# A new plan of instruction order for a linear-attention and feed-forward kernel on one Trainium2 core

## The chip, the cores and the metric

The kernel runs on one core of one Trainium2 chip. The metric is the device time of one execution in microseconds (us). Most executions of one kernel agree within a few tenths of a per cent, but chips differ by about one per cent: in the four sets of rounds used here, on three chips or more, the kernel before took 191.03, 193.21, 192.01 and 192.41 us. Kernels are compared by a ratio: the mean time of one kernel's fast runs over the mean time of the other kernel's fast runs of the same rounds on the same chip. It is not quite the ratio of the medians that are quoted. A run more than 1.5% above the fastest of its kernel counts as slow and stays out of the ratio. Each ratio has a 95% interval. All "spans" are those of one profiled execution.

## The reference, cut to what matters

```python
# r, k, v: (4 batches, 8 heads, 768 steps, 48), float32; w, u: (8, 48)
for t in range(S):
    cur = u * k_t (outer) v_t
    y[t] = r_t @ (state + cur)
    state = w * state + k_t (outer) v_t
x = y as (3072 tokens, 384)
h = x @ w_in                  # (384, 2048)
out = relu(h) ** 2 @ w_out    # (2048, 384)
```

The kernel cuts time into chunks of 128 steps: 6 chunks by 4 batches make 24 **units**, chunk by chunk. Per unit it scales r and k by powers of the decay, transposes both, forms masked scores (eight matrix products), y (scores times v plus r times the old state), and the new state. Two units make a **pair** for the feed-forward part: 8 groups of six w_in products and twice 8 groups of two w_out products for each of 12 pairs.

## The kernel before

The kernel lists every operation with its engine, an assumed cost and a key. A function plays the list through in an imaginary clock and so fixes the order in which each engine's queue receives its instructions. "S" is the sync queue, which issues loads, DMA transposes and stores; "D" is the DMA engines; "T", "V", "A", "P" are TensorE, VectorE (DVE), ScalarE (ACT) and GpSimd (POOL). The clock in this plan is only the kernel's own idea of time; the chip runs by semaphores.

```python
        cost = o.eng[e]                      # in schedule(): one shared port of V and P
        if e == "V" and o.port and last["P"] is not None and last["P"].end > s and last["P"].port:
            cost += 0.4
...
    NLOAD, NPADS = 8, 4                      # 8 buffers each for k, r and v tiles
    NT = 10                                  # from unit 10 on, transposes go by DMA
    NDVE = 6                                 # from unit 6 on, the products are GpSimd's alone
...
        full = [(loads[-4], 0.0)] if len(loads) >= 4 else []
        behind = [(loads[-1].go, 0.0)] if loads else []
        q[nm + "_go"] = op(f"ld_{nm}{n}", {"S": 0.45}, PACE * (n - AHEAD), full + behind + [gate], f, takes=[q["_" + nm]], lat=0.8)
        q[nm] = op(f"{nm}{n}", {"D": 0.88}, PACE * (n - AHEAD), [q[nm + "_go"]], lambda e: None, lat=0.75)
...
    w_ops = []                               # four units, then w_in and w_out by turns, then the rest
    for i in range(len(PIECES) - 1):
        for which in ("in", "out"):
            w_ops.append(weights(i, which, w_ops[-3] if len(w_ops) >= 3 else units[2]["vt"]))
...
            q["go_t"] = op(                  # DMA transpose of the scaled r and k of a unit
                f"go_t{n}", {"S": 0.5}, K + 1, [q["rw"]],
                lambda e, T=T: nc.sync.dma_start_transpose(...), takes=[X["rkT"]], uses=[X["krp"]], lat=0.8)
...
                q["smo"] = op(f"smo{n}", both(0.96, 0.48), K + 5, [q["sma"]],      # decay of the state: 128 x 384
                              tt(lambda sm=sm: SM(sm), lambda sm=sm: SM(sm), lambda: wc, ALU.mult), uses=[sm], port=True)
...
                o_go = op(f"go_x{q['n']}", {"S": 0.5}, PACE * q["n"] + 4.4, [q["yb"]],   # DMA transpose of y into xt
                          lambda e, XT=XT, i=i, q=q: nc.sync.dma_start_transpose(...), ...)
            o_m = op(f"m1.{j}.{f}", {"T": 0.655}, key, o_xt + [o_win[f]], m1, ...)       # a w_in group
                prev[i] = op(f"m2.{j}.{i}.{f}", {"T": 0.325}, key + LAG + 0.2 * i, ...)  # a w_out group
            o_st = op(f"st{q['n']}", {"S": 0.5}, KM + PACE * (L + i) - 30, [o_o], ...)   # store, sync queue only
```

## Time and profile before

| | before |
|---|---|
| time, median (lowest to highest) | 191.03 us (190.22 to 191.9) |
| span of the profiled execution | 188.4 us |
| first w_in product | 19.46 us |
| last w_in group starts | 181.74 us |
| TensorE's work, by the spacing of starts | 147.3 us, of it 143.8 after the first w_in product |
| TensorE without work after the first w_in product | 21.3 us |

A product is charged its own spacing in a dense row (0.109 us for one of w_in, 0.163 for one of w_out), and what is left between two starts is a hole. Half-speed clock counts as hole too. Two lines of the view of the waits (engine, line, tile, the releaser; then us in total, times, longest):

```profile
POOL krp L290 <- DMA kt<-in_k_dram: 8.9, 1, 8.9
PE bank L559 <- DMA xt<-yb: 3.5, 1, 3.5
```

The first is GpSimd standing still for unit 4's k, loaded behind all weights. The second is TensorE standing still at 94 us for the transposed y tile of unit 11.

### The profile page before, as it was taken

The numbers are of one execution on the slowest core, as the hardware profiler recorded it, in microseconds if no ns is written. First come the engines' busy times: TensorE is split into PE (matmuls) and PEld (weight loads), VectorE is DVE, ScalarE is ACT, GpSimd is POOL, SyncE is SP. The second block draws the span as 40 slices with busy tenths as digits, with TensorE's granted clock in tenths as the row PEclk, the third lists the DMA queues.
The fourth block names the chain that finished last, engine by engine and source line by source line (L and its number), as shares of the span: only waits on it lengthen the run. The fifth ranks groups of instructions, "written<-read, shape, count | busy, mean of one in ns | idle before, by whom it ended". The sixth has DMA issues, their size and how long they took to land.

```text
span 188.4 us, 4319 instructions
## 1 busy us (share of the span) xinstructions
PE 170.1 (90%) x1643; PEld 121.9 (65%) x1643; DVE 135.0 (72%) x229; ACT 110.2 (58%) x197; POOL 128.2 (68%) x144
## 2 busy tenths in 40 slices
PE   6997778869979999799839999999999999999992
PEld 2753555657767867577526767777777777777760
DVE  6579985569877777778605879788687776874741
ACT  4565654459787597567603645677565564464641
POOL 2588751089999989989908799999999993000000
PEclk9999999999999999999966999999999999999999
DMA  5999999999899999998894898406433424030202
GB/s 111 214 219 132 125 184 161 196 179 245 174 232 230 201 218 207 206 216 173 208 191 94 210 175 199 123 0 153 88 80 121 94 64 122 0 108 23 83 3 85
DMA packets 103256, 27.56 MB, mean 146 GB/s; under 512 B 96065, under 2 KB 103234, under 8 KB 103234
## 3 DMA queue, kind: packets, MB, share of 16 engines
q1 hardware_dynamic: 99088, 24.13, 58.4%
q0 software_dynamic: 4128, 3.15, 12.2%
q8 instruction: 13, 0.21, 0.5%
q14 instruction: 9, 0.07, 0.1%
q10 hardware_dynamic: 18, 0.00, 0.0%
HBM read 20.65 MB, written 4.72 MB: 135 GB/s over the span
## 4 chain that ended last, share of the span: by engine, by line
PE 54%; DMA 20%; POOL 13%; SPq 5%; issue 3%; DVE 2%; ACT 1%; POOLq 0%
PE bank L588 24%; PE bank L559 22%; DMA w_out_sb<-in_moe_w_out_dram 6%; POOL krp L290 5%; SPq L356 4%; DMA kt<-in_k_dram 4%; DMA w_in_sb<-in_moe_w_in_dram 3%; PE bank L483 3%; POOL rk L290 2%; POOL rku L290 2%; DMA vt<-in_v_dram 2%; DMA rt<-in_r_dram 2%; POOL dv L290 2%; DMA rkT<-krp 2%; PE bank L507 2%
## 5 line engine op out<-in xcount | busy, mean ns | idle before, releaser
L559 PE MATMUL bank<-xt,w_in_sb 128*128 128x256 bf16 x576 | 79.1, 276 | 6.7 <-DMA xt<-yb 3.5
L588 PE MATMUL bank<-w_out_sb,g 128*128 128x384 bf16 x384 | 81.2, 329 | 0.1
L579 ACT ACTIVATE g<-gr 128x512 bf16<-128x512 f32 x92 | 57.9, 630 | 36.9 <-DVE gr L571 36.1
L571 DVE TENSOR_SCALAR gr<-bank 128x512 f32<-128x512 f32 x73 | 50.4, 691 | 32.1 <-PE bank L559 27.3
L559 PEld LDWEIGHTS <-w_in_sb 128*128 128x128 bf16 x576 | 55.3, 99 | 21.8 <-DMA xt<-yb 3.9
L588 PEld LDWEIGHTS <-g 128*128 128x128 bf16 x384 | 34.4, 98 | 15.4 <-ACT g L579 0.6
L491 DVE TENSOR_TENSOR AT<-bank,smask 128x512 bf16<-128x512 f32 x48 | 30.8, 682 | 2.4 <-PE bank L483 1.9
L290 POOL TENSOR_TENSOR rk<-rt,kt 128x384 f32<-128x384 f32 x24 | 24.7, 1027 | 4.2 <-DMA rt<-in_r_dram 4.2
L290 POOL TENSOR_TENSOR krp<-kt,wk 128x384 bf16<-128x384 f32 x19 | 19.0, 1002 | 8.9 <-DMA kt<-in_k_dram 8.9
L290 POOL TENSOR_TENSOR krp<-rt,wr 128x384 bf16<-128x384 f32 x22 | 22.6, 1026 | 1.0 <-DVE krp L290 1.0
L295 ACT CAST vb<-vt 128x384 bf16<-128x384 f32 x24 | 12.3, 511 | 16.4 <-PE bank L507 9.6
L290 POOL TENSOR_TENSOR rku<-rk,ub 128x384 f32<-128x384 f32 x21 | 21.2, 1011 | 0.2
L290 POOL TENSOR_TENSOR dv<-vb,du 128x384 f32<-128x384 bf16 x20 | 17.0, 848 | 4.1 <-DVE du L422 4.1
L573 ACT ACTIVATE gr<-bank 128x512 f32<-128x512 f32 x23 | 13.7, 595 | 6.0 <-PE bank L559 5.5
L515 DVE TENSOR_TENSOR yb<-bank,dv 128x384 bf16<-128x384 f32 x24 | 13.3, 553 | 5.0 <-PE bank L507 4.1
L290 POOL TENSOR_TENSOR sm<-sm,wc 128x384 f32<-128x384 f32 x15 | 15.0, 999 | 1.7 <-DVE sm L290 1.6
L422 DVE TENSOR_REDUCE du<-rku 128x8 f32<-128x384 f32 x24 | 13.0, 543 | 0.5 <-POOL rku L290 0.4
L483 PE MATMUL bank<-rkT 48*128 48x128 bf16 x192 | 10.0, 222 | 2.6 <-DMA rkT<-krp 1.4
L507 PE MATMUL bank<-vb,AT 128*128 128x48 bf16 x192 | 11.5, 186 | 0.4 <-DVE AT L491 0.4
L507 PEld LDWEIGHTS <-AT 128*128 128x128 bf16 x192 | 10.0, 98 | 2.2 <-issue 1.1
L483 PEld LDWEIGHTS <-rkT 48*128 48x128 bf16 x192 | 5.7, 95 | 8.6 <-issue 4.1
L295 ACT CAST sb<-sm 128x384 bf16<-128x384 f32 x20 | 10.1, 505 | 1.7 <-DVE sm L290 1.5
(54 smaller groups left out, 137.8 us busy)
## 6 DMA issues: line engine op xcount, KB each, us to landing
kt<-in_k_dram SPq DMA_DIRECT2D x24, 192.0 KB, 3.7
rt<-in_r_dram SPq DMA_DIRECT2D x24, 192.0 KB, 3.6
vt<-in_v_dram SPq DMA_DIRECT2D x24, 192.0 KB, 3.7
out_dram<-osb SPq DMA_DIRECT2D x24, 192.0 KB, 2.4
w_in_sb<-in_moe_w_in_dram POOLq DMA_DIRECT2D x3, 384.0 KB, 6.6
w_out_sb<-in_moe_w_out_dram POOLq DMA_DIRECT2D x3, 384.0 KB, 7.0
w_in_sb<-in_moe_w_in_dram POOLq DMA_DIRECT2D x2, 192.0 KB, 4.6
w_out_sb<-in_moe_w_out_dram POOLq DMA_DIRECT2D x2, 192.0 KB, 4.3
```

The source lines that it names most:

```text
L290: return lambda e: NOW[e].tensor_tensor(dst(), a(), b_(), f)
L295: nc.scalar.copy(dst(), src())
L422: lambda e, T=T: nc.vector.tensor_reduce(T("du"), T("rku"), axis=mybir.AxisListType.X, op=ALU.add),
L483: nc.tensor.matmul(out=psv(at[i], NP, C)[:, p, :], lhsT=T("rkT")[rows, 1, p, :], rhs=T("rkT")[rows, 0, p, :], start=True, stop=True,)
L491: lambda e, T=T, i=i, x=x: nc.vector.tensor_tensor(T("AT")[:, i], psv(x, NP, C), smask[:, None, :].to_broadcast([128, NP, C]), ALU.mult),
L507: nc.tensor.matmul(out=t[:, p, i, :], lhsT=T("AT")[:, i, p, :], rhs=T("vb")[:, 2 * p + i, :], start=st is None, stop=True, skip_group_chec ...
L515: lambda e, T=T, y_p=y_p: nc.vector.tensor_tensor(T("yb"), psv(y_p, HD), T("dv").rearrange("t h d -> t (h d)"), ALU.add),
L559: nc.tensor.matmul(out=psv(h, 2, L * C)[:, z], lhsT=w_in_sb[:, kk, (2 * f + z) * 128 : (2 * f + z + 1) * 128], rhs=XT()[:, kk].rearrange(" ...
L571: nc.vector.tensor_scalar(dst, src, 0.0, None, ALU.max)
L573: nc.scalar.activation(dst, src, AF.Relu)
L579: nc.scalar.activation(dst, src, AF.Square)
L588: nc.tensor.matmul(out=psv(o_p, dm), lhsT=G()[:, 2 * f + z, i, :], rhs=w_out_sb[:, 2 * f + z, :], start=(f == 0 and z == 0), stop=(f == NH ...
```

## The change

The intent is to give each queue an order that the chip can follow without holes. The plan gets a model of DMA in phases (issue, transfer, completion), true queue costs, stalls for instruction fetches and an exclusive port for DVE and GpSimd; the order is then tuned by a table of 189 entries that override key, engine or earliest place of single operations. Beside that the kernel itself changes: w_in comes in one stretch and w_out in another, loads are paced by the scores of three units earlier, stores may go by ACT's queue, the state is stored densely, early decay tables lie in PSUM, and the u product uses full height. Smaller parts: DMA transposes begin with unit 8 instead of 10, the first two w_in groups of the first two pairs are split by unit, and TensorE starts with more products of zeros (48 instead of 19).

```diff
-def schedule(ops, depth, limits, free, away, warm_until):
+def schedule(ops, depth, limits, free, away, stalls, warm_until=0.0, cold=0.0):
...
+                if e == "V" and o.port:
+                    for a, b in heldP[-6:]:
+                        if s < b and s + cost > a:
+                            s = b                       # wait instead of paying for overlap
...
+        if o.dma is not None:
+            pre, xf, post = o.dma
+            x0 = max(s + pre, free["D"])
+            x1 = x0 + xf + sum(d for at, d in stalls if x0 <= at < x0 + xf)
...
-    NT = 10
-    NDVE = 6
+    NT = 8
+    NDVE, RUN = 24, 3
+    NUDGE = {
+        "vt0": (0.0, None, 5.57), "rt4": (0.0, None, 26.62), "vt8": (0.0, None, 51.18), ...   # (key, engine, earliest)
+        "m1.11.6": (0.0, None, 170.12), "m1.11.7": (0.0, None, 173.84),
+    }
+    FEED = (("units", 0, 4), ("in", 0, 5), ("units", 4, 6), ("out", 0, 5), ("units", 6, NU))
...
-        q[nm + "_go"] = op(f"ld_{nm}{n}", {"S": 0.45}, ...)
+        q[nm] = op(f"{nm}{n}", {"S": 0.58}, PACE * (n - AHEAD), deps, f, takes=[q["_" + nm]], lat=0.05, dma=(1.75, 0.92, 0.7))
...
-                f"go_t{n}", {"S": 0.5}, K + 1, [q["rw"]],
+                f"rkT{n}", {"S": 1.24}, K + 1, [q["rw"]],
...
-                q["smo"] = op(f"smo{n}", both(0.96, 0.48), K + 5, [q["sma"]],
+                q["smo"] = op(f"smo{n}", both(0.55, 0.32), K + 5, [q["sma"]],      # 128 x 192 now
...
+        if n + RUN < NU and n + RUN >= 6:                # a load is planned after the scores three units before
+            for nm in ("kt", "rt", "vt"):
+                units[n + RUN][nm].deps.append((q["am"], 0.0))
...
-            o_st = op(f"st{q['n']}", {"S": 0.5}, ...)
+            op(f"st{q['n']}", {"S": 0.45, "A": 0.5}, ...)
...
+        if o.after is not None:                          # GpSimd waits for the DVE product placed before it
+            tc.add_manual_dep(o.made.ins, o.after.made.ins.name, LANDED)
```

## The prediction

> **What bounds the kernel now.** I read the page from the top (shares, the forty slices), then the chain of waits, then a table of stretches, then the timeline where that table shows a hole. First the shares and the slices of the page:
>
> ```profile
> PE 170.1 (90%) x1643; PEld 121.9 (65%) x1643; DVE 135.0 (72%) x229; ACT 110.2 (58%) x197; POOL 128.2 (68%) x144
> PE   6997778869979999799839999999999999999992
> POOL 2588751089999989989908799999999993000000
> PEclk9999999999999999999966999999999999999999
> DMA  5999999999899999998894898406433424030202
> ```
>
> TensorE is the engine at its limit, but in two different ways. From slice 22 on its digits are nines without a hole; before that there are sevens and eights, and one 3 (slice 20, near 95 us) with a granted clock of 6 tenths beside it. GpSimd is at nine tenths from slice 8 to 33 and idle afterwards; the DMA engines are full in the first 20 slices. The early half is thus fed too slowly, and the late half pays back a backlog.
>
> The chain that ended last, in order of time, gives the price of one piece of TensorE work when nothing is missing, and what leads the chain early:
>
> ```profile
> 24.68 6.20 DMA w_out_sb<-in_moe_w_out_dram
> 30.89 7.40 DMA kt<-in_k_dram
> 38.44 1.00 POOL krp L290
> 43.71 0.65 PE bank L559 x6
> 44.36 0.65 PE bank L588 x4
> 104.77 0.33 PE bank L483 x8
> 182.56 2.36 PE bank L588 x14
> 184.94 0.56 DVE osb L297
> ```
>
> Six w_in products take 0.65 us (0.109 each), four w_out products 0.65 us (0.163 each), the eight score products of a unit 0.33 us. With 576 and 384 of them, the feed-forward part costs 576 x 0.109 + 384 x 0.163 = 62.8 + 62.6 = 125.4 us. Adding, for all 24 units, scores, y, state and transposes by the same spacing of starts, I get 147 us of TensorE work in a span of 188.4. So some 41 us are idle or slowed: about 19 before the first w_in product (19.46 us) and the other 22 after it. The stretches show where:
>
> ```profile
> 20.00:40.00 20.00, 14.96 (x134) 10.41 (x132) 13.96 (x22) 10.49 (x17) 8.09 (x10) 1.00 1.06 164
> 94.00:97.50 3.50, 0.01 (x2) 0.01 (x1) 0.57 (x1) 0.15 (x1) 0.39 (x1) 0.72 0.99 200
> 97.50:102.40 4.90, 4.90 (x30) 3.32 (x31) 1.45 (x3) 0.51 (x1) 2.56 (x3) 0.50 0.69 140
> 130.00:160.00 30.00, 30.00 (x300) 22.24 (x299) 21.84 (x37) 17.71 (x32) 26.99 (x29) 1.00 0.41 104
> ```
>
> The columns are busy time with counts of PE, PEld, DVE, ACT and POOL, then granted clock, DMA share, GB/s. From 20 to 40 us starts are missing for 6.6 us (by spacing); from 94 to 97.5 there is nothing at all; from 97.5 to 102.4 the clock is 0.50, which costs half of 4.9, about 2.4 us. From 130 on it is dense. Slices 40 to 80 us add 4.6 us of small waits. The hole in detail, in the timeline:
>
> ```profile
> 93.56 1.48 SPq L447 DMA_TRANSPOSE rkT<-krp  x1
> 95.15 1.20 SPq L539 DMA_TRANSPOSE xt<-yb  x1
> 97.49 0.13 PEld L559 LDWEIGHTS <-w_in_sb 128*128 128x128 bf16 x2 [3.88 <-DMA xt<-yb]
> ```
>
> The y tile it transposes was written by DVE at 89.44 to 90.0. Its transpose was issued at 95.15, because the sync queue first worked off another transpose, three loads and the transpose shown: each transpose holds that queue 1.2 to 1.5 us, while the old plan books 0.5. This stall is a wrong order in one queue, not a lack of engine time.
>
> **What the Trainium skill says.** "TensorE: Matmul & The Clock Gate", Part 1: about 3.4 us of idleness sends the array back to half clock. The trace agrees: a wait of 3.49 us, then 0.50. "GPSIMD Engine Reference", section Key points: GpSimd shares its SBUF interfaces with VectorE and contends with DVE instructions that have two SBUF inputs. The trace agrees: a DVE product of 128x384 takes 0.54 us at 19.48, but 1.37 and 1.43 us at 20.41 and 22.30, beside a GpSimd product. "DMA: Bandwidth & Descriptors", Specifications: line rate wants at least 512 B per transfer; here 96,065 of 103,256 packets are under 512 B, and full DMA engines move 164 GB/s in 20 to 40 us. "Runtime: NRT & Kernel Launch", Instruction fetch mechanics: instructions are refilled in 16 KiB blocks by the sequencer's own DMA queue; the page shows 13 packets with 0.21 MB on an instruction queue, and the new plan lists 13 stalls of the DMA engines. No view shows what one of these costs.
>
> **The change, part by part.** Most of it is the order of the instructions on each queue; the total of useful work hardly moves.
>
> 1. *Weights in one stretch.* Now: four units, ten weight pieces alternating w_in and w_out, then unit 4, whose k lands at 38.4 us. TensorE has two pairs' feed-forward but waits for each piece: 1.35 us at 32.15, 1.88 at 37.44 and the rest of the 6.6. New: four units, all w_in, units 4 and 5, then all w_out. Unit 4 comes about 9 to 13 us earlier, so GpSimd does not stand still for 8.87 us as in the waits view. Against it, no second product can run before w_out; the plan names a release of 37.05 for a w_out product of the first pair (now the first runs at 22.07). Releases in the change are earliest places in the order in the plan's own clock, no hardware waits. The fourth w_in group of the third pair is released at 52.13; in the trace that group starts at 57.64. I take 4 of these 5.5 us.
>
> 2. *DMA phases and true queue costs.* A transpose is now booked at 1.2 us on the sync queue, a load at 0.58, and x transposes get 1 us of slack. This should remove the hole at 94 and with it the slow clock: 3.5 + 2.4 = 5.9 us. As two more units are transposed by DMA (from unit 8, not 10), TensorE loses 2 x (8 + 3) transposes x 0.056 = 1.2 us, ACT and DVE the copies; the sync queue gains 4 issues. I give back 1 to 2 us for smaller new waits of this kind.
>
> 3. *Exclusive port, GpSimd or DVE for all units.* GpSimd's work per unit is now 1.03 + 1.03 + 1.01 + 1.00 + 0.85 + 1.00 = 5.9 us, against TensorE's 10.45 / 2 + 0.33 + 0.37 + 0.17 = 6.1 us; a near tie, which is why one late unit in the middle delays TensorE. The dense state halves the elements of the decay product (0.55 booked, not 1.00), over 16 units about 7 us less GpSimd; the plan may now also place any of these products on DVE (135 of 188 us busy). The price is small instructions: the state sum and the cast become two of 64 partitions each, some 0.1 and 0.2 us more per unit on DVE and ACT, which are not the limit. Added waits of GpSimd on the preceding DVE instruction should be met already. Gain: part of the 4.6 us of 40 to 80, say 1 to 2.
>
> 4. *Start.* Eight products for the decay columns (1.7 us of PE) disappear, the decay tables in PSUM keep ten DVE products off the shared port, the u product uses 128 rows instead of one (same 1.64 us). GpSimd gains a large memset, but its first product is at 6.19 now. Against it stand releases of 20.06 and 21.55 for the y transposes of units 0 and 1 (trace: 15.52 and 18.55). I count 0.
>
> 5. *End.* After the last w_in group starts (181.74) the rest takes 188.4 - 181.74 = 6.7 us: relu, square, w_out, copy, store. It cannot shrink much.
>
> Sum: 4 + 5.9 - 1.5 + 1.5 = 9.9 us from the parts. The plan itself offers a second estimate: the last w_in group is released at 173.84, 7.9 us before its place in the trace; with the same end the span is 180.5. I take 8.6 us, between the two and nearer the plan: 191.1 - 8.6 = 182.5 us (times lie 2.7 us above the traced span).
>
> **Rivals.** *TensorE turns into the only limit*: then 147 - 1 us of work, 4 us of it before 22 us, gives 22 + 142 + 3.5 = 168 for the span, 171 for the time. Against it speaks that w_out arrives only near 35 us and the plan's own releases near 174; I don't expect it. *The hole moves*: the order on each queue is frozen by a plan with hundreds of hand-set keys; one transpose in the wrong place again costs 3.5 us and perhaps a slow-clock window of up to 3.4 more, leaving 187 to 189. The present hole shows that this happens; the corrected queue costs speak against it. *Early starvation*: holding w_out back leaves TensorE with two pairs of w_in products (10.5 us) and units until about 36; over 3.4 us idle there halves the clock, which gives 185 to 188. *Backlog only*: if the late stretch were dense regardless, an earlier middle would gain nothing; but a dense tail pulls forward by just as much as its start does, so holes are worth their length.
>
> **Range and chances.** 182.5 us, 8 in 10 between 178.5 and 188. Low end: both estimates and the 2% that the plan books too much for TensorE (0.668 per w_in group, 0.654 here) come in. High end: one new hole with slow clock. Chances: 0.86 faster by over 2% (under 187.3), 0.12 within 2%, 0.02 slower.
>
> **What would show it.** Right: no wait on the x transpose over 1 us after 60 us, PEclk at nine or ten throughout, the last w_in group near 174, unit 4's k landing near 25 us, GpSimd without its 8.87 us wait, no DVE product over 1 us beside GpSimd. Wrong: TensorE idle between 25 and 37 for w_out, a clock of 0.5 in a new place, GpSimd waiting for DVE in place of DVE being slowed, or long waits on transposes queued behind loads.

## The result, and the profile after

| | before | after |
|---|---|---|
| time, median of 4 runs (lowest to highest) | 191.03 us (190.22 to 191.9) | 180.64 us (180.11 to 181.13) |
| ratio, 95% | | 0.9457 [0.9411, 0.9503] |
| span | 188.4 us | 178.9 us |
| mean granted clock of TensorE | 0.962 to 0.991 (24 fast runs of the experiments' rounds) | 1.000 in all 4 runs |

The gain is 10.4 us against the 8.6 predicted. From the page of the changed kernel, the shares and the slices (a digit is the busy share of a fortieth of the span in tenths):

```profile
PE 168.4 (94%) x1682; PEld 119.9 (67%) x1684; DVE 138.8 (78%) x262; ACT 105.7 (59%) x214; POOL 112.7 (63%) x136
PE   7899899959999999999999999999999999899991
POOL 7449726710499588965795698999799855220200
PEclk9999999999999999999999999999999999999999
```

Counting slices from 0, TensorE has nines from slice 9 to 38 but for one eight, the clock row has no dip, and GpSimd is no longer at nine tenths in nearly every slice of the middle. The stretches of the changed kernel (busy time and count of PE, PEld, DVE, ACT, POOL, then granted clock, DMA share, GB/s):

```profile
20.00:40.00 20.00, 17.20 (x223) 13.77 (x221) 17.73 (x35) 16.12 (x32) 8.66 (x12) 1.00 1.06 168
60.00:80.00 20.00, 20.00 (x202) 14.30 (x199) 16.84 (x34) 11.44 (x25) 16.37 (x19) 1.00 0.96 180
80.00:100.00 20.00, 20.00 (x214) 14.89 (x212) 18.44 (x35) 14.62 (x30) 13.23 (x17) 1.00 0.96 184
```

The stretch from 80 to 100, which held the hole, is busy from end to end; so is 60 to 80. The longest losses of TensorE, and GpSimd's wait for a k tile, are in the view of the waits:

```profile
POOL krp L405 <- DMA kt<-in_k_dram: 4.2, 1, 4.2
PE bank L737 <- DMA w_out_sb<-in_moe_w_out_dram: 2.1, 1, 2.1
PE bank L703 <- DMA xt<-yb: 1.4, 2, 1.0
```

and in the chain that ended last (start, us, what):

```profile
31.82 7.80 DMA w_out_sb<-in_moe_w_out_dram
39.66 1.46 PE bank L737 x8
121.87 5.10 DMA xt<-yb
170.86 0.65 PE bank L703 x6
171.51 3.27 PE bank L737 x20
```

TensorE waits once for w_out, 2.1 us before 39.66, and the clock stays at 1.00. The transpose of 5.10 us in the chain costs TensorE little: its longest wait for a transposed y tile is 1.0 us. The last w_in group starts at 170.69 instead of 181.74 by the starts of its products (the chain counts it from 170.86), and 22 w_out products start after it instead of 14 (the last piece of the chain holds 20 of the 22).

Where the 9.5 us of span came from is seen best in TensorE's holes, by spacing of starts, from the first w_in product (19.46 us before, 19.75 after):

| stretch, us | holes before | holes after | gain |
|---|---|---|---|
| to 40 | 6.6 | 4.8 | 1.8 |
| 40 to 80 | 4.6 | 1.9 | 2.7 |
| 80 to 105 | 7.3 | 1.1 | 6.2 |
| 105 to 140 | 1.4 | 1.7 | -0.4 |
| 140 to the end | 1.4 | 2.2 | -0.8 |
| sum | 21.3 | 11.8 | 9.5 |

TensorE's work after its first w_in product is nearly the same (143.8 and 143.2 us). (The gains are taken before rounding; another choice of the dense spacing moves single cells by a few tenths.) So the whole gain is holes of TensorE that have closed, and two thirds of it lies between 80 and 105 us, where the hole at 94 and the slow clock after it were.

What the table doesn't tell is which part of the change closed them. That took the experiments.

### The profile page after: what moved, and what is told of

It is laid out like the page before. It is cut to its first block, busy times and chain, and to the rows that moved or that the text cites. A ratio compares the mean times of both kernels' runs of the same rounds, so it can differ in the third digit from the quotient of the medians.

```text
span 178.9 us, 4423 instructions
## 1 busy us (share of the span) xinstructions
PE 168.4 (94%) x1682; PEld 119.9 (67%) x1684; DVE 138.8 (78%) x262; ACT 105.7 (59%) x214; POOL 112.7 (63%) x136
## 4 chain that ended last, share of the span: by engine, by line
PE 60%; DMA 21%; SPq 4%; POOL 4%; DVE 4%; issue 3%; ACT 1%; POOLq 0%; DVEq 0%
PE bank L737 27%; PE bank L703 26%; DMA rt<-in_r_dram 7%; DMA xt<-yb 5%; DMA w_in_sb<-in_moe_w_in_dram 5%; DMA w_out_sb<-in_moe_w_out_dram 4%; SPq L470 4%; PE bank L622 3%; DVE gr L720 2%; PE bank L649 2%; PE bank L644 1%; PE bank L582 1%; POOL rk L405 1%; POOL w_in_sb L489 1%; POOL w_out_sb L491 1%
## 5 line engine op out<-in xcount | busy, mean ns | idle before, releaser
L703 PE MATMUL bank<-xt,w_in_sb 128*128 128x256 bf16 (+1 forms) x600 | 74.7, 268 | 2.0 <-DMA xt<-yb 1.4
L728 ACT ACTIVATE g<-gr 128x512 bf16<-128x512 f32 x84 | 51.5, 629 | 25.5 <-DVE gr L720 23.6
L720 DVE TENSOR_SCALAR gr<-bank 128x512 f32<-128x512 f32 x65 | 44.2, 689 | 14.7 <-PE bank L703 13.5
L730 POOL TENSOR_TENSOR g<-gr 128x512 bf16<-128x512 f32 x12 | 12.5, 1039 | 19.7 <-DVE gr L720 17.6
L405 POOL TENSOR_TENSOR rk<-rt,kt 128x384 f32<-128x384 f32 x17 | 17.0, 1002 | 4.6 <-DMA rt<-in_r_dram 4.6
L614 ACT CAST sb_all<-sm 64x192 bf16<-64x192 f32 x40 | 13.9, 348 | 8.9 <-POOL sm L405 8.5
L405 POOL TENSOR_TENSOR krp<-rt,wr 128x384 bf16<-128x384 f32 x16 | 16.0, 999 | 1.9 <-DVE krp L405 1.5
L398 PE MATMUL bank<-zb 128*128 128x512 bf16 x48 | 14.0, 416 | 1.5 <-DVE zb L307 1.2
L410 ACT COPY osb<-bank 128x384 f32<-128x384 f32 x17 | 7.8, 478 | 11.1 <-PE bank L737 11.1
L600 DVE TENSOR_TENSOR sm<-bank,sm 64x192 f32<-64x192 f32 x32 | 11.3, 352 | 2.1 <-PE bank L582 1.8
```

The lines of the kernel that those rows point to most:

```text
L398: nc.tensor.matmul(out=banks[7], lhsT=zb[:, :128], rhs=zb, start=True, stop=True, skip_group_check=True)
L405: return lambda e: NOW[e].tensor_tensor(dst(), a(), b_(), f)
L410: nc.scalar.copy(dst(), src())
L614: halves(lambda e, rows, i, sb=sb, sm=sm: nc.scalar.copy(SM(sb)[rows, :, i, :], SM(sm)[rows])),
L703: nc.tensor.matmul(out=out_, lhsT=w_in_sb[:, kk, (2 * f + z) * 128 : (2 * f + z + 1) * 128], rhs=rhs, start=(kk == 0), stop=(kk == NK - 1) ...
L720: nc.vector.tensor_scalar(dst, src, 0.0, None, ALU.max)
```

## The experiments

**Theory**: the holes were a fault of the joint order on the queues. The sync queue, which alone issues the DMA transposes, was filled with loads up to eight units ahead, and a late transpose starves TensorE. The first four expectations still hold the prediction's simpler cause, one wrong order at the hole; the loads came in with the fifth, after the first results. **Rivals**: (a) single parts carry it: true queue costs, or weights in one stretch, or the slow clock; (b) GpSimd was the limit, and the dense state or the exclusive port freed it; (c) TensorE is simply bound, and any plan would do. The first four ran on one chip, the next four on a second, the last four on a third.

### Moving one transpose forward (kernel before)

```diff
+    by_name = {o.name: o for o in placed}
+    moved = [by_name[x] for x in ("go_x11", "ld_kt20", "ld_rt20", "ld_vt20")]
+    placed = [o for o in placed if o not in moved]
+    at = placed.index(by_name["yb11"]) + 1
+    placed[at:at] = moved
```

> The kernel before with one move in the sync queue: the x transpose of unit 11 is issued ahead of the other transpose and of the three loads of unit 20 that stood before it; every compute engine keeps its order. Theory (queue order made the hole): the transpose is issued near 91.4 us instead of 95.15, TensorE waits under 0.5 us instead of 3.5 for it, the clock stays at 1.0, and 4 to 6 us go: 185 to 187. Rival (the hole is lack of engine work, the transposed tile would only wait for something else): the wait moves to another releaser, gain under 1 us, 190 to 191.

Measured: 191.49 us against 193.21, ratio 0.9904 [0.9819, 0.9989]. The profile fell in a run counted as slow (span 191.8), so only the place of its hole is used. The wait at 94 is gone; in the view of the waits there is another of the same kind:

```profile
PE bank L559 <- DMA xt<-yb: 3.1, 1, 3.1
```

It begins at 111.48 us, one pair later, and TensorE's clock falls to 0.66 between 115 and 120. So the hole moved. Repairing one queue position is worth about 1.9 us by the ratio (0.2 to 3.5 by its interval), not the 5.9 of the hole and the slow clock: the hole is the visible end of a debt that the sync queue carries along.

### Keeping the array busy in the hole (kernel before)

```diff
             def m1(e, f=f, h=h, XT=XT, j=j):
+                if (j, f) == (5, 0):
+                    for _ in range(17):
+                        nc.tensor.matmul(out=psv(h, 512), lhsT=zb[:, :128], rhs=zb, start=True, stop=True, ...)
```

> The kernel before, with 17 products of zeros (3.6 us at full clock) put in front of the first w_in group of the sixth pair, into the bank that this group then overwrites; the transpose still comes late. Theory (the slow clock is a second cost that comes from TensorE's idleness): clock 1.0 from 97.5 to 102, gain of 2 to 2.4 us of the 5.9, so 188.7. Rival (the slow clock came by chance or costs nothing as other engines bound that stretch): 190.5 to 191.2.

Measured: 190.28 us, 0.9865 [0.9805, 0.9925], some 2.6 us (1.4 to 3.8 by the interval). The stretch that had the slow clock:

```profile
98.00:103.00 5.00, 4.95 (x42) 3.13 (x41) 1.59 (x3) 0.67 (x2) 1.32 (x2) 1.00 0.86 173
```

The clock is 1.00 where the kernel before had 0.50, though the transposed tile came no earlier (its transpose was issued at 97.65 us). The slow clock is thus a cost of its own beside the hole, and its measured size agrees with the prediction's 2.4 us. That idleness brings half clock is what the Trainium skill says in Part 1 of "TensorE: Matmul & The Clock Gate"; the length that it gives is taken up in the last section.

### Weights in the new order alone (kernel before)

```diff
-        for which in ("in", "out"):
-            w_ops.append(weights(i, which, w_ops[-3] if len(w_ops) >= 3 else units[2]["vt"]))
+    for what, lo, hi in (("units", 0, 4), ("in", 0, 5), ("units", 4, 6), ("out", 0, 5), ("units", 6, NU)):
+        if what == "units": ...   # load(n, nm, after)
+        else: ...                 # weights(i, what, loads[-4])
```

> The kernel before with the loads in the new order: four units, all of w_in, units 4 and 5, all of w_out, the rest; nothing else. Theory (weights in one stretch are worth about 4 us on the early half): unit 4 arrives near 28 us instead of 38, the third pair's first w_in group starts 3 to 5 us earlier than 53.56, and 187 if the later half keeps the lead, more if a hole like that near 94 eats it. Rival (w_out held back starves TensorE as much as it helps): third pair at 53 us or later, 190 to 192.

Measured: 194.81 us, 1.0099 [1.0011, 1.0187]; a loss. The third pair starts a little earlier (52.55 us instead of 53.56), but at 93 us TensorE waits longer than ever:

```profile
PE bank L560 <- DMA xt<-yb: 8.1, 2, 7.3
```

The early lead was eaten at the next fault of the order. By itself this part is worth nothing.

### True queue costs alone (kernel before)

```diff
-                f"go_t{n}", {"S": 0.5}, K + 1, [q["rw"]],
+                f"go_t{n}", {"S": 1.24}, K + 1, [q["rw"]],
-                o_go = op(f"go_x{q['n']}", {"S": 0.5}, ...
+                o_go = op(f"go_x{q['n']}", {"S": 1.2}, ...
-        q[nm + "_go"] = op(f"ld_{nm}{n}", {"S": 0.45}, ...
+        q[nm + "_go"] = op(f"ld_{nm}{n}", {"S": 0.58}, ...
```

> The kernel before with only the booked costs of the sync queue corrected in its plan: 1.24 and 1.2 us for transposes instead of 0.5, 0.58 for loads instead of 0.45. Theory (true queue costs are what removes the hole): the wait on the x transpose near 94 us is gone or under 1 us, 185 to 188. Rival (the old plan is off in more than these costs, so the order stays as bad): another hole of 2 us or more on a transpose, 189 to 193.

Measured: 190.48 us, 0.9857 [0.9781, 0.9932], about 2.7 us. A shorter hole is left, from 98.09 us on:

```profile
PE bank L559 <- DMA xt<-yb: 2.5, 1, 2.5
```

TensorE stands still for 2.47 us by this line, and the stretch of 98 to 103 us has a clock of 0.78; microsecond by microsecond it is 1.00 until 100 and 0.50 from 101 on. So a hole of 2.5 us was enough for the slow clock here, less than the 3.4 us that the prediction took from the skill.

Among the parts this is rival (a)'s best, and it gives a quarter of the gain; the verdict "faster by over 2%" is not reached. The plan's own end did not notice either the fault or its repair: it is 171.8 us in the plan's clock with the old costs and with the new ones, against traced spans of 188.4 and 189.3.

### Pacing the loads alone (kernel before)

```diff
+    for n in range(8, NU):            # only the places of the loads in the queue
+        for nm in ("kt", "rt", "vt"):
+            o = by_name[f"ld_{nm}{n}"]
+            users = [placed.index(x) for x in units[n]["_" + nm].users if x is not o and ...]
+            to = min(placed.index(by_name[f"am{n - 4}"]), min(users) - 1)
+            if placed.index(o) < to:
+                placed.remove(o); placed.insert(to, o)
```

> The kernel before, compute engines in the same order, but from unit 8 on each unit's three loads stand in the sync queue just ahead of the scores of the unit four before it, not up to eight units ahead. New theory (the hole near 94 us is a debt: from 60 to 80 us the sync queue issued 18 loads for units up to eight ahead and only one transpose, so units came late in the DMA stage and any single move only shifts the hole): both holes of over 2 us go and 3 to 6 us with them, ratio to before 0.97 to 0.985. Rival (the sync queue and DMA engines have too much to do whenever loads are issued): hole as long or longer, ratio 0.99 to 1.01.

Measured: 199.3 us, 1.0378 [1.0327, 1.043]. My theory expected a gain, and got a loss of 7.3 us. The waits show why:

```profile
ACT vb L295 <- DMA vt<-in_v_dram: 29.2, 13, 5.4
PE bank L588 <- ACT g L579: 9.0, 6, 2.7
```

ScalarE's old order casts v as early as the old loads brought it. With later loads it stands 29.2 us in 13 waits (6.5 in 7 before), and what stands behind the casts in its queue comes late too: TensorE waits 9.0 us for its squares. So this run doesn't test the sync queue alone. Pacing is no gain in itself; it must fit the order of the other queues.

### Loads as early as buffers allow (changed kernel)

```diff
+    for n in range(8, NU):
+        for nm in ("kt", "rt", "vt"):
+            o = by_name[f"{nm}{n}"]
+            old = [placed.index(x) for x in units[n - 8]["_" + nm].users] + [placed.index(by_name[f"am{n - 7}"])]
+            to = max(old) + 1
+            if placed.index(o) > to:
+                placed.remove(o); placed.insert(to, o)
```

> The changed kernel, compute engines in the same order, but each load from unit 8 on is moved forward in the sync queue to where its buffer comes free, so up to seven or eight units ahead as in the kernel before. New theory (loads too early): transposes are issued late between 60 and 100 us, at least one TensorE wait of 2 us or more on a transpose appears, ratio to before 0.96 to 0.98 instead of 0.946. Rival (pacing does not matter, the order of the transposes does): below 1 us lost, ratio 0.945 to 0.952.

Measured: 198.64 us, 1.0309 [1.0222, 1.0396]; its profile is of a slow run. It shows a fault of my edit: loads of unit 8 got ahead of those of units 4 to 7, and TensorE had nothing to do for 9.85 us from 41.42 on. This tells nothing of the theory; it was repeated in a cleaner form, further down.

### All stores on the sync queue (changed kernel)

```diff
             op(f"st{q['n']}", {"S": 0.45, "A": 0.5}, ...      # the plan books them as before
-               lambda e, osb=osb, row=row: (nc.sync if e == "S" else nc.scalar).dma_start(
+               lambda e, osb=osb, row=row: nc.sync.dma_start(
```

> The changed kernel with all 24 stores issued from the sync queue, at the same places in the plan (17 of them go through ScalarE's queue in the changed kernel). Rival theory S (what the change gained is room in the sync queue): 17 x 0.45 us more for that queue, transposes late, 2 to 4 us lost, ratio 0.955 to 0.968. If the pacing is what matters: under 1 us, ratio up to 0.952.

Measured: 184.0 us, 0.9546 [0.9471, 0.962], against 0.9457 for the changed kernel: about 0.9% lost, though the intervals overlap. TensorE's waits for transposed y tiles grow from 1.4 us in two to

```profile
PE bank L703 <- DMA xt<-yb: 3.1, 4, 1.2
```

That fits the Trainium skill, section Rules for kernel authors of "DMA: Bandwidth & Descriptors": issuing from several engines saves the sequencer's issue time alone. Here that time would be what is short on the sync queue; the overlap of the intervals leaves it unproven. The transposes cannot be spread in the same way: the section DMA Transpose (X-bar) of that page says that transposes from two queues in flight together can corrupt each other silently. No run here tried it.

### Without the table (changed kernel)

```diff
-        shift, only, o.release = NUDGE.get(o.name, (0.0, None, 0.0))
+        shift, only, o.release = (0.0, None, 0.0)
```

> The changed kernel without its table of hand-set keys, engines and releases; the plan is computed from the same costs. If the costs of the plan (queues, port, DMA) are the gain, it stays within 2.5 us of the changed kernel, ratio 0.946 to 0.96. If the table is the gain, 5 us or more are lost, ratio over 0.97. The plan's own end is 187.1 instead of 182.6, so by that 4.5 us lost.

Measured: 190.11 us, 0.9884 [0.9826, 0.9941]: 4.3%, some 8 us, are lost with the table alone, all other parts of the change in place. The wait and the stretches:

```profile
PE bank L582 <- POOL krp L405: 5.0, 2, 4.3
76.00:81.00 5.00, 0.67 (x14) 0.46 (x10) 1.67 (x4) 1.31 (x4) 5.00 (x7) 0.76 0.52 144
81.00:88.00 7.00, 6.19 (x59) 4.46 (x58) 4.04 (x8) 3.15 (x6) 5.96 (x8) 0.69 0.62 104
```

TensorE stands for 4.33 us from 76.28 on, this time for a product of GpSimd, which is busy 5.00 us of 5.00, and pays with a clock of 0.69 afterwards. With no table the plan leaves GpSimd 128.2 us of work, as before; the table's choices of DVE for some products are part of its 112.7 in the changed kernel. Rival (c), that any plan with this model will do, falls.

### Loads early, in clean order (changed kernel)

```diff
+    last = by_name["vt9"]
+    for n in range(10, NU):           # loads keep their order among themselves; compute orders are untouched
+        for nm in ("kt", "rt", "vt"):
+            o = by_name[f"{nm}{n}"]
+            old = [...users of the buffer...] + [placed.index(by_name[f"am{n - 6}"])] + [placed.index(last)]
+            to = max(old) + 1
+            if placed.index(o) > to:
+                placed.remove(o); placed.insert(to, o)
+            last = o
```

> The changed kernel with every compute engine in the same order; from unit 10 on each unit's three loads stand in the sync queue after the scores of the unit six before it (about three before, in the changed kernel), and stay in their own order. The run a_early had put unit 8's loads ahead of those of units 4 to 7 and so starved unit 5; this one can't. Theory (loads too far ahead take the queue and the DMA engines from the transposes): the transposes issue late between 55 and 100 us, at least one TensorE wait over 1.5 us on what they bring, ratio to before 0.955 to 0.975. Rival (pacing is worth nothing in the changed kernel): ratio 0.944 to 0.950.

Measured: 194.0 us, 0.9999 [0.991, 1.0088]. With the table, the costs, the weights' order and the rest in place, moving only loads from unit 10 on to up to six units ahead loses the whole gain, more than I had expected. Two of the four runs count as slow, so the ratio rests on two (190.93 and 193.59 us). The profile is of a fast run. The sync queue in its timeline (start, duration, what was issued):

```profile
60.90 0.95 SPq L470 DMA_DIRECT2D vt<-in_v_dram  x1
61.94 0.70 SPq L470 DMA_DIRECT2D kt<-in_k_dram  x1
62.69 1.31 SPq L470 DMA_DIRECT2D rt<-in_r_dram  x1
64.06 0.72 SPq L470 DMA_DIRECT2D vt<-in_v_dram  x1
64.89 3.07 SPq L564 DMA_TRANSPOSE rkT<-krp  x2
```

and that of the changed kernel:

```profile
56.70 1.33 SPq L564 DMA_TRANSPOSE rkT<-krp  x1
58.09 0.57 SPq L470 DMA_DIRECT2D rt<-in_r_dram  x1
58.70 0.58 SPq L470 DMA_DIRECT2D vt<-in_v_dram  x1
59.45 1.50 SPq L564 DMA_TRANSPOSE rkT<-krp  x1
```

In the first, twelve loads go out in a row from 52.83 to 64.78 us and both transposes follow; in the second, the transposes come at 56.70 and 59.45, with two or three loads between. TensorE's answer in the first:

```profile
68.59 0.61 PE L622 MATMUL bank<-rkT 48*128 48x128 bf16 x8 [6.34 <-DMA rkT<-krp]
```

6.34 us of standing still for the transposed tile, and the stretch 60 to 80 has a clock of 0.83. Its source, the scaled r and k of unit 8, was complete at 56.20 us in GpSimd's timeline, 8.7 us before the transpose was issued at 64.89; from issue to landing the two transposes took 2.8 and 3.7 us, against a median of 4.2 in the changed kernel. So what came late was the issue, not the transfer. This is the shape of the hole of the kernel before, made at will by the place of loads in one queue. As to the cause of such holes the theory holds. How large the loss is holds for this order alone: all other queues are fitted to the paced loads.

### GpSimd not held for DVE (changed kernel)

```diff
-        if o.after is not None:
+        if False:
             tc.add_manual_dep(o.made.ins, o.after.made.ins.name, LANDED)
```

> The changed kernel without the added waits of GpSimd on the VectorE product before it; same order on all engines. If the exclusive port is a gain by itself on the chip: VectorE products of two SBUF inputs go from 0.55 to over 1 us beside GpSimd again, 1 to 3 us lost, ratio 0.951 to 0.962. If the waits are met anyway or cost as much as they save: ratio 0.943 to 0.950.

Measured: 183.53 us, 0.9544 [0.95, 0.9588], about 0.9% or 1.6 us lost, with an interval that just touches that of the changed kernel. By tile, the DVE products of r and k with u (shortest, median and longest in ns) in this kernel:

```profile
L405 DVE TENSOR_TENSOR rku<-rk,ub x7: 548/550/1350, 7.6 to 86.7; 128x384 f32<-128x384 f32 x7
```

One of them takes 1350 ns and one product of r with k 1154; in the changed kernel the longest of the first are 552 and of the second 693. The wait does what it is meant to do: two engines that would slow each other take turns.

### Doubling the decay product (changed kernel)

```diff
+                def decay2(e, sm=sm):
+                    NOW[e].tensor_tensor(spare, wc, wc, ALU.mult)      # a second product of the same size
+                    return NOW[e].tensor_tensor(SM(sm), SM(sm), wc, ALU.mult)
```

> The changed kernel with the decay product of the dense state doubled: beside each of the 16 products of 128x192 a second one into a tile that nobody reads, on the same engine; the order is kept. It puts back the GpSimd work that the dense state saved, about 14 x 0.6 = 8 us, and 2 x 0.35 on VectorE. My step 3 (GpSimd and TensorE nearly tied, so this work is worth 1 to 2 us): ratio 0.950 to 0.957. Rival (GpSimd has room, 63% busy): no change, 0.944 to 0.949. Rival 2 (GpSimd is the limit of the middle): 5 us or more, over 0.97.

Measured: 181.61 us, 0.9458 [0.9402, 0.9513], no change against 0.9457. GpSimd had 14 products more:

```profile
PE 169.5 (94%) x1682; PEld 120.2 (67%) x1684; DVE 140.5 (78%) x264; ACT 105.9 (59%) x214; POOL 118.8 (66%) x150
```

6.1 us more of GpSimd cost nothing. As this run puts back about what the dense state took away, the dense state is worth nothing measurable in this order (the two intervals leave about 1.4 us open). Rival (b) falls as the main cause; of it the exclusive port's 0.9% may remain.

### A table searched further

```diff
-    NUDGE = { ...189 entries, as in the change... }
+    NUDGE = { ...760 entries, found by a random search that lowers the plan's own end from 182.6 to 180.9... }
```

> The changed kernel with a table of keys, engines and releases found by going on with a random search over the plan's own end: the plan ends at 180.9 instead of 182.6; costs and instructions are the same. If the plan's end is a true guide to about 1 us: 1 to 2 us faster than the changed kernel, ratio 0.935 to 0.941. If the search has only fitted the plan's errors: ratio 0.946 or more.

Measured: 183.17 us, 0.9533 [0.9488, 0.9578]; no faster than the changed kernel and probably slower; its stand-in on this chip is the run above (181.61 us, 0.9458 [0.9402, 0.9513], whose interval overlaps a little). The plan promised 1.7 us less, and the medians are 1.5 us apart the other way. The plan's end and the traced span: 182.6 and 178.9 for the changed kernel, 180.9 and 180.4 here, 187.1 and 187.1 without the table. The new plan is true to some 4 us, where the old one was 17 us too short (171.8 for 188.4), but a search that asks it for less than those 4 us fits its errors. No version was found that beats the changed kernel.

All runs that gave a clean reading, together (left out is the first form of loads early, 1.0309, for the fault of its edit):

| kernel | what | ratio to before |
|---|---|---|
| before | one transpose forward | 0.9904 |
| before | busy array in the hole | 0.9865 |
| before | weights in one stretch | 1.0099 |
| before | true queue costs | 0.9857 |
| before | paced loads | 1.0378 |
| after | as it is | 0.9457 |
| after | loads early | 0.9999 |
| after | no table | 0.9884 |
| after | stores on one queue | 0.9546 |
| after | GpSimd not held | 0.9544 |
| after | decay product doubled | 0.9458 |
| after | searched further | 0.9533 |

## Why the prediction was right, and where it was not

The prediction was right in direction, in range and in the main mechanism: holes of TensorE close, nothing else of weight happens. Its single steps fared differently, and the cause it gave for the largest hole failed.

- **What bounds the kernel**: right. Of 21.3 us of holes 9.5 closed, and the gain in the span is 9.5. Two readings were off without consequence. The 41 idle us are about 16 before the first w_in product (19.46 less 3.5 of work) and 25 after it, of which 21.3 are holes and 3.9 the end, not 19 and 22. And GpSimd's row is not at nine tenths throughout slices 8 to 33: slice 20, that of the hole, has a 0.
- **Part 1, weights in one stretch (4 us)**: too large, and with the wrong measure. The group whose release the text used did come earlier: matched to the trace by the plan's order, it starts at 53.30 instead of 57.64 us (it is now the sixth of its pair; the fourth starts at 50.19). But that is order, not gain: TensorE ran w_in groups in place of w_out ones. In holes, the stretch to 40 us gained 1.8. As a single part on the old kernel it lost 1%.
- **Part 2, queue costs (5.9 us, less 1 to 2 given back)**: the size was right, the holes between 80 and 105 us shrank by 6.2, and only 1.2 came back after 105. The clock part was right to 0.2 us (2.6 measured, 2.4 predicted), though the wait of 3.49 us did not come first and the 0.50 after it: the clock was at 0.50 from 95.5 us on, 1.5 us into the hole, as the 0.72 in the text's own line for 94.0 to 97.5 shows. The step that failed is the cause, as the text put it: "a wrong order in one queue". One reordering moved the hole by a pair, and true queue costs alone gave 1.4% (about 2.7 us). The runs showed in its place a joint order: where loads stand between transposes (up to 5.7% of the changed kernel's time, 0.9999 over 0.9457), together with a table that fits the other queues to it (4.5% in the same measure, 0.9884 over 0.9457). The text did not price the paced loads at all; taking them out of the finished order cost more than any other part that was tried.
- **Part 3, GpSimd near a tie (1 to 2 us)**: the stretch 40 to 80 did gain 2.7 us. The dense state, which the text made the main reason, is worth nothing measurable by the doubled product; the exclusive port is worth 1.6 us by its run, if that difference is real. That GpSimd can hold up TensorE is shown by the run without the table (4.33 us).
- **Part 4, start (0)**: right in sum, first w_in product at 19.75 instead of 19.46 us. "Same 1.64 us" for the u product does not fit this trace: its two passes start 0.40 us apart instead of 0.80. The height is not the reason. In the three traces with the new product in which the clock's record of full speed begins before 5 us (as it is, the first loads early, stores on one queue) the passes are 0.39 to 0.40 us apart; in the four in which it begins after 6 us (no table, loads early, not held, doubled) they are 0.77 to 0.78 apart. So it is the state of the clock.
- **Part 5, end (6.7 us)**: it grew to 8.2 us (178.9 less 170.69). 22 instead of 14 w_out products were left to do after the last w_in group; eight at 0.163 us are 1.3 of the 1.5.
- **The plan as a second estimate**: the last w_in group was released at 173.84 in the plan's clock and started at 170.69 in the trace; the prediction leaned towards the plan, and the sum of parts (9.9 us) would have been nearer.
- **Rivals**: early starvation came true in the small, 2.1 us for w_out before 39.66 us, and the clock did not fall. "The hole moves" did not happen in the changed kernel, but in four experiments (one transpose forward, weights alone, no table, loads early). TensorE as the only limit is not reached, 11.8 us of holes are left.
- **Signals**: the longest wait on a transposed y tile is 1.0 us, the clock row is even, and no DVE product takes 0.9 us or more. Unit 4's k was issued at 24.43 us and its product starts at 28.54, so it landed some 3.5 us later than the 25 named, but 10 earlier than before. GpSimd's wait of 8.87 us for it is gone; the 4.2 us in the view of the waits come at 44.60 and are for unit 6, whose loads now stand behind w_out.

What stays open: that the sum of the parts comes so near to the whole is partly luck, as the parts don't add (1.4%, nothing and losses one by one, 5.4% together). Which of the table's entries matter was not tried, nor were the instruction fetch model, the split first w_in groups and the longer start with zeros. The two costs of 0.9% rest on intervals that touch or overlap that of the changed kernel.

## What to carry to other kernels

When loads and latency-bound transfers share one issuing queue, count the queue's own time per issue and ask, for every transfer that the busiest engine waits for, how many issues stand ahead of it: loads ahead of their need are not free. A hole that vanishes at one place should be looked for one step later before its length is booked as a gain, and a part that loses alone may still be needed by the whole. A plan may be searched as far as its error against the trace, and no further.

## What the Trainium skill lacked or had wrong

- "DMA: Bandwidth & Descriptors", section Issuing engines are not separate DMA queues, calls the time to issue a DMA on the sequencer usually small beside the transfer. Here one DMA transpose of scaled r and k held its queue for 1.30 us by the median of 16 in the changed kernel (1.23 to 2.58), beside 4.2 us from issue to landing, and a 192 KB load for 0.5 to 0.7 us and at times 1.3 or more. A queue with 12 loads ahead of a transpose cost TensorE 6.34 us; no page that I read warns of that.
- "TensorE: Matmul & The Clock Gate", Part 1, gives about 3.4 us of idleness as the bound before half clock. The mechanism agrees (2.6 us were gained by keeping the array busy), the length does not. In the kernel before, the clock was at 0.50 from 95.5 us on, 1.5 us after TensorE had stopped at 94.0. In the kernel with true queue costs a hole of 2.47 us was followed by 0.50; in the changed kernel one of 2.1 us was not. So a hole well below 3.4 us can bring half clock. From which length on, these runs don't settle.
